# Second MLP of an attention, mixture-of-experts and MLP kernel: two tiles' activations turned on TensorE, the token rows of tiles 3 on turned through DRAM and 32x32 VectorE transposes

## The chip, the cores and the metric

One core of a Trainium2 chip runs the whole program. The time is the device time of one execution in microseconds (us), and the figure for a kernel is the median of its runs. The engines are TensorE (PE, with its weight loads shown apart as PEld), VectorE (DVE), ScalarE (ACT), GpSimd (POOL) and SyncE (SP, which only issues DMAs here). Each engine takes its instructions in the order in which the kernel writes them.

## The reference, cut to what matters

Attention comes first, then a layer of 8 experts with two of them for each token, then a second MLP over all 2304 tokens. The change touches the expert layer's last sum and the MLP:

```python
out[mask] += top2_w[mask, k, None] * (h @ w2[e])      # two expert rows for each token

h = x @ w_in                                          # 2304x512 @ 512x1024
e = np.exp(h - h_max)
sm = e / (np.sum(e, axis=-1, keepdims=True) + 1e-09)
solu = h * sm
mu, var = mean(solu), mean((solu - mu) ** 2)          # over the 1024 features
ln = (solu - mu) / np.sqrt(var + 1e-06) * g_ln
return ln @ w_out                                     # 2304x1024 @ 1024x512
```

All matrices are float32. The kernel splits each operand into a high and a low part (fp32r) and forms three products.

## The kernel before, in words

The 2304 tokens are 18 tiles of 128 tokens. In the MLP stage, a tile has its tokens on the 128 partitions and its features along the free dimension. A matrix product contracts over partitions, so both the tile's 512 input features and its 1024 activations have to be turned (features to partitions) before `h_in` and before `o_out`.

The stage is one loop over `i` (L1172). Each line of its body serves another tile, and nothing but the order written here sets the order on the engines (the schedule is manual):

- `h_in(i)` is 48 matmuls of 256 columns on PE (L840), into one of two PSUM buffers.
- `d_read(i-1)` reads the activations of tile i-1 back from DRAM with four DMAs on SP, so that each 32x32 block lies where a block transpose needs it. It waits until the write `d_write(i-1)` has landed.
- `d_back(i-2)` turns them: a DVE 32x32 block transpose of 128x1024 (L896), an ACT cast to the high part (L899), a DVE subtraction for the low part (L900).
- `x2_trans(i+1)` turns the input row of tile i+1: four PE transposes (L732), an ACT cast from PSUM (L734), a DVE subtraction (L735).
- `solu(i)` is a DVE maximum (L849), an ACT exponential (L852), a DVE product (L855), a DVE subtraction of the mean (L858), with small column operations (L853, L854, L856) between them.
- `d_write(i)` sends the result to DRAM.
- `combine(i+3)` adds the two expert rows of tile i+3: an ACT scaling (L822) and a DVE multiply-add (L823).
- `rstd(i-1)` is an ACT square with a sum (L868) and a chain of small DVE and ACT operations (L870 to L878).
- `o_out(i-3)` is 24 matmuls of 512 columns on PE (L923), an ACT copy out of PSUM (L928) and the store.
- `gather_y(i+5)` gathers expert rows with two indirect DMAs from POOL.

Tiles 16 and 17 do not go through DRAM: `d_trans` turns them with eight PE transposes each, two ACT casts (L913) and two DVE subtractions (L914), from activations that L860 has put in the column order of the DRAM path (partition 32g+c of chunk k holds feature 256g+32k+c). `w_out` is loaded in that order with four DMAs for each piece (L156); `w_in` is loaded in the plain order with one (L146). `combine(0)` to `combine(2)` and `x2_trans(0)`, `x2_trans(1)` stand ahead of the loop, between the last expert's products; `x2_trans(2)` stands in iteration 0.

Of the kernel before, what the change touches and what calls it, by code (L numbers as in the profile page):

```python
# [8 lines left out]
F32 = mybir.dt.float32  # L9
F32R = mybir.dt.float32r  # L10
# [10 lines left out]
NT, DM, FF, E = 2304, 512, 1024, 8  # L21
R = 4
NC = NT // 128
NL = S - 128 * R
KD, KF = DM // 128, FF // 128
# [22 lines left out]
def col_rows(t):  # L48

    j, c = divmod(t, 9)  # L50
    if c == 8:
        return [(64 * u, 64, (2 * j + u) * S + 128 * R, 1) for u in range(2)]
    return [(0, 128, (2 * j + c // R) * S + c % R, R)]

ORDER = """
F:100011101100000000100000000000101111 lk:0 lq:0 lkl:0 lk:1 kr:0 kmt:0 qm:0 lvl:0 km:0:0 klt:0 kl:0 km:0:1 kb:0
# [26 lines left out]
def attn_moe_kernel(ctx: ExitStack, tc: tile.TileContext, q, k, v, w_gate, w_noise, noise,  # L83
                    w1, w2, w_in, w_out, g_ln, out, order=None, stop=False):
    nc = tc.nc
    V, A, P, T, SP = nc.vector, nc.scalar, nc.gpsimd, nc.tensor, nc.sync
# [5 lines left out]
    dram = ctx.enter_context(tc.tile_pool(name="dram", bufs=1, space=DRAM))  # L92
    sb = ctx.enter_context(tc.tile_pool(name="sb", bufs=1))

    def slot(tag, shape, dt, name):
        return sb.tile(shape, dt, tag=tag, name=name)

    def ring(*tags):
        state = [-1]

        def take(shape, dt, name):
            state[0] = (state[0] + 1) % len(tags)
            return slot(tags[state[0]], shape, dt, name)
        return take

    new_raw = ring("R2", "R3", "R0", "R1")
    new_row = ring("S0", "S2", "S4", "S1", "S3")
    new_out = ring("S9", "S8", "S10")
    new_s2 = ring("S5", "S6", "S7", "S11")
# [6 lines left out]
    tab = dram.tile([OVT * 128, 2], I32, name="tab")  # L116
    win32 = dram.tile([DM, FF], F32, name="win32")
    wout32 = dram.tile([FF, DM], F32, name="wout32")
    dd = [dram.tile([128, FF], F32, name=f"dd{t}") for t in range(NC - 2)]

    def bank_t():
        return psT.tile([128, 512], F32, tag="t", name="t")
# [4 lines left out]
    def bank_b():  # L127
        return psB.tile([128, 512], F32, tag="b", name="b")
# [13 lines left out]

    def load_w1(e, j):
        t = new_raw([128, KD, 256], F32, "raw")
        src = win32 if e == E else w1[e]
        SP.dma_start(out=t, in_=src[:, 256 * j:256 * j + 256].rearrange("(k p) f -> p k f", p=128))  # L146
        raw[1, e, j] = t

    def load_w2(e, j):
# [116 lines left out]
    RH = {}  # L266
# [462 lines left out]
    def transpose_split(t, hi, lo):  # L729
        ps = bank_t()  # L730
        for kk in range(KD):
            T.transpose(ps[:, 128 * kk:128 * kk + 128], t[:, 128 * kk:128 * kk + 128], ident)  # L732
        pv = ps.rearrange("p (k t) -> p k t", k=KD)
        A.copy(hi, pv)  # L734
        V.tensor_sub(lo, pv, hi)  # L735
# [62 lines left out]
    yg, x2r, x2T, hb, dT, rsd = {}, {}, {}, {}, {}, {}  # L798
# [4 lines left out]
    def col_of(t):  # L803

        return t if t < NC - 2 else 2 * NC - 3 - t
# [13 lines left out]
    def combine(t):  # L819
        a, b = yg.pop((t, 0)), yg.pop((t, 1))  # L820
        c = col_of(t)
        A.activation(out=a, in_=a, func=AF.Copy, scale=gw[:, c, 0:1])  # L822
        V.scalar_tensor_tensor(a, b, gw[:, c, 1:2], a, op0=OP.mult, op1=OP.add)  # L823
        x2r[t] = a

    def x2_trans(t):
        a = x2r.pop(t)
        hi = new_s2([128, KD, 128], F32R, "x2h")
        lo = new_s2([128, KD, 128], F32R, "x2l")
        transpose_split(a, hi, lo)  # L830
        x2T[t] = (hi, lo)

    def h_in(t):
        hi, lo = x2T.pop(t)
        pa = bank_a()
        for n in range(2):
            for kk in range(KD):
                for s, (x, w) in enumerate(((hi, W1h), (hi, W1l), (lo, W1h))):
                    for c in range(2):
                        T.matmul(pa[:, n, 256 * c:256 * c + 256], lhsT=x[:, kk, :],  # L840
                                 rhs=w[2 * n + c][:, kk, :], start=(kk == 0 and s == 0 and c == 0),
                                 stop=(kk == KD - 1 and s == 2), skip_group_check=True)
        hb[t] = pa

    def solu(t):
        pa = hb.pop(t)
        c = col[:, t]
        pf = pa.rearrange("p n f -> p (n f)")
        V.reduce_max(c[:, 0:1], pf, axis=AX, negate=True)  # L849
        ed = new_ed([128, 2, FF], F32, "ed")  # L850
        e, d = ed[:, 0], ed[:, 1]
        A.activation(out=e, in_=pf, func=AF.Exp, bias=c[:, 0:1], accum_out=c[:, 1:2])  # L852
        V.tensor_scalar(c[:, 2:3], c[:, 1:2], 1e-9, None, op0=OP.add)  # L853
        V.reciprocal(c[:, 2:3], c[:, 2:3])  # L854
        V.scalar_tensor_tensor(d, pf, c[:, 2:3], e, op0=OP.mult, op1=OP.mult, accum_out=c[:, 3:4])  # L855
        V.tensor_scalar(c[:, 4:5], c[:, 3:4], -1.0 / FF, None, op0=OP.mult)  # L856
        if t < NC - 2:
            V.tensor_scalar(d, d, c[:, 4:5], None, op0=OP.add)  # L858
        else:
            V.tensor_scalar(e.rearrange("p (k g c) -> p g k c", g=4, k=KF), d.rearrange(  # L860
                "p (g k c) -> p g k c", g=4, k=KF), c[:, 4:5], None, op0=OP.add)
            e, d = d, e
        rsd[t] = e, d, c[:, 7:8]
# [20 lines left out]
    def d_write(t):  # L884
        SP.dma_start(out=dd[t], in_=rsd[t][1])

    def d_read(t):
        x = dq[t] = new_dq([128, 2, FF], F32, "dq")
        for g in range(4):
            SP.dma_start(out=x[32 * g:32 * g + 32, 0].rearrange("i (b f) -> i b f", b=4),  # L890
                         in_=dd[t].rearrange("(b i) f -> i b f", i=32)[:, :, 256 * g:256 * g + 256])

    def d_back(t):
        x = dq.pop(t)
        xt = x[:, 1].rearrange("p (k b i) -> p k b i", k=KF, b=4)
        V.transpose(xt.rearrange("p k b i -> p b k i"), x[:, 0].rearrange("p (b k c) -> p b k c", b=4, k=KF))  # L896
        xt = xt.rearrange("p k b i -> p k (b i)")
        dt = new_dT([128, 2, KF, 128], F32R, "dT")
        A.copy(dt[:, 0], xt)  # L899
        V.tensor_sub(dt[:, 1], xt, dt[:, 0])  # L900
        dT[t] = (dt[:, 0], dt[:, 1])

    def d_trans(t):
        d = rsd[t][1]
        dt = new_dT([128, 2, KF, 128], F32R, "dT")
        for i in range(2):
            ps = bank_t()
            for k in range(4):
                c = 512 * i + 128 * k
                T.transpose(ps[:, 128 * k:128 * k + 128], d[:, c:c + 128], ident)  # L910
            pv = ps.rearrange("p (k t) -> p k t", k=4)
            hi, lo = (dt[:, j, 4 * i:4 * i + 4, :] for j in range(2))
            A.copy(hi, pv)  # L913
            V.tensor_sub(lo, pv, hi)  # L914
        dT[t] = (dt[:, 0], dt[:, 1])

    def o_out(t):
        hi, lo = dT.pop(t)
        pb = bank_b()
        for kk in range(KF):  # L920
            wh, wl = (w[:, kk % 2, :] for w in WO[kk // 2])
            for s, (x, w) in enumerate(((hi, wh), (hi, wl), (lo, wh))):
                T.matmul(pb, lhsT=x[:, kk, :], rhs=w, start=(kk == 0 and s == 0),  # L923
                         stop=(kk == KF - 1 and s == 2))
        y = rsd.pop(t)[2]
        o = new_out([128, DM], F32, "o")
        if t < NC - 1:
            A.activation(out=o, in_=pb, func=AF.Copy, scale=y)  # L928
        else:
            A.activation(out=o[:, 0:256], in_=pb[:, 0:256], func=AF.Copy, scale=y)  # L930
            V.tensor_scalar(o[:, 256:512], pb[:, 256:512], y, None, op0=OP.mult)  # L931
        for p0, n, row, st in col_rows(col_of(t)):
            dst = out[row:row + n, :] if st == 1 else out[row - row % S:row - row % S + st * n, :].rearrange(
                "(p r) d -> p r d", r=st)[:, row % S, :]
            SP.dma_start(out=dst, in_=o[p0:p0 + n, :])
# [232 lines left out]
    x2_trans(1)  # L1168
    A.preload_act_table_set(ACT_SET)
    combine(2)  # L1170
    split_w2(E, 2)
    for i in range(NC + 3):  # L1172
        if i < NC:
            h_in(i)
        if 0 <= i - 1 < NC - 2:
            d_read(i - 1)
        if 0 <= i - 2 < NC - 2:
            d_back(i - 2)
        if 2 <= i < NC - 1:
            x2_trans(i + 1)  # L1180
        if i < NC:
            solu(i)
        if i < NC - 2:
            d_write(i)
        if i == 0:
            x2_trans(2)
        if i < NC - 3:
            combine(i + 3)
        if i == 1:
            split_w2(E, 3)  # L1190
        if 1 <= i <= NC:
            rstd(i - 1)
        if i >= 3:
            o_out(i - 3)
        if i in (NC - 1, NC):
            d_trans(i - 1)
        if i + 5 < NC:
            gather_y(i + 5)
# [31 lines left out]
```

## Time and profile before

| | |
|---|---|
| median of 3 runs | 815.04 us (814.2 to 815.2) |
| the profiled execution | 813.08 us, span 811.3 us |
| PE busy | 756.5 us, 93% of the span |
| PEld busy | 682.5 us, 84% |
| DVE busy | 504.0 us, 62% |
| ACT busy | 293.9 us, 36% |
| POOL busy | 147.1 us, 18% |
| granted TensorE clock, mean | 0.981 of 2.4 GHz |

The span runs from the first to the last instruction; the execution's time includes 1.8 us around it. A busy share is an average over stages. The MLP loop takes the last 220 us of the span.

### The profile page before, as it was taken

The page shows a single profiled execution, that of the slowest core. Times are in us where ns is not written, and L with a number is a line of the kernel's source. Part 1 is how long each engine was busy: PE and PEld are TensorE (multiplying, and loading weights), DVE is VectorE, ACT ScalarE, POOL GpSimd, SP SyncE. Part 2 cuts the span into 40 slices and gives each one's busy share as a digit, 9 for nine tenths or more (in the row PEclk, how much of TensorE's full clock was granted, in tenths as well). Part 3 has the DMA queues.
Part 4 walks back from the last instruction along what each step waited for, and adds up shares of the span by engine and source line. Part 5 has one row for each costly group of instructions (what it writes and reads, how often), then busy time and mean ns, then how long its engine had stood idle before and what let it go on. Part 6 is the DMA issues. An engine that isn't in the chain of part 4 may idle for free. (4 is left out here: it accounts for less than half of the span.)

```text
span 811.3 us, 12471 instructions
## 1 busy us (share of the span) xinstructions
PE 756.5 (93%) x4918; PEld 682.5 (84%) x4918; DVE 504.0 (62%) x884; ACT 293.9 (36%) x484; POOL 147.1 (18%) x130
## 2 busy tenths in 40 slices
PE   2877859999999999999999999999988999999997
PEld 1776858989889889899899899898777999899986
DVE  5899783335656656657646656555466777767661
ACT  1566531333223223223232332231444444444441
POOL 3584563020110110200100200000341211200000
PEclk9998899999999999999999999999997999999999
DMA  9973444264454443554544452532754645543311
GB/s 266 269 249 118 143 158 143 79 195 156 134 178 130 144 157 129 170 168 128 177 137 141 170 168 79 162 119 90 219 167 156 179 151 164 156 144 130 107 50 39
DMA packets 82974, 122.07 MB, mean 150 GB/s; under 512 B 15072, under 2 KB 53984, under 8 KB 82912
## 3 DMA queue, kind: packets, MB, share of 16 engines
q1 hardware_dynamic: 76832, 101.32, 39.3%
q0 software_dynamic: 6080, 19.93, 8.7%
q8 instruction: 39, 0.64, 0.3%
q14 instruction: 23, 0.19, 0.1%
HBM read 88.72 MB, written 32.51 MB: 149 GB/s over the span
## 5 line engine op out<-in xcount | busy, mean ns | idle before, releaser
L756 PE MATMUL a<-xh,w1h 128*128 128x320 f32 x448 | 138.6, 309 | 1.2 <-DVE hl L761 1.2
L756 PE MATMUL a<-xl,w1h 128*128 128x320 f32 x448 | 138.4, 309 | 0.0
L756 PE MATMUL a<-xh,w1l 128*128 128x320 f32 x448 | 138.4, 309 | 0.0
L792 PE MATMUL b<-w2h,hh 128*128 128x512 f32 x320 | 128.8, 402 | 0.0
L792 PE MATMUL b<-w2h,hl 128*128 128x512 f32 x320 | 126.7, 396 | 0.0
L792 PE MATMUL b<-w2l,hh 128*128 128x512 f32 x320 | 126.3, 395 | 0.0
L760 ACT ACTIVATE hh<-a 128x640 fp32r<-128x640 f32 x56 | 39.5, 706 | 159.9 <-PE a L756 159.9
L725 POOL DMA_INDIRECT xg<-xd,idx x38 | 40.7, 1070 | 304.1 <-PE t L732 294.7
L761 DVE SCALAR_TENSOR_TENSOR hl<-a,hh 128x640 fp32r<-128x640 f32 x56 | 46.1, 823 | 64.8 <-ACT hh L760 64.8
L756 PEld LDWEIGHTS a<-xh,w1h 128*128 128x128 f32 x448 | 84.1, 188 | 1.8 <-DVE hl L761 1.4
L756 PEld LDWEIGHTS a<-xl,w1h 128*128 128x128 f32 x448 | 84.1, 188 | 0.4
L756 PEld LDWEIGHTS a<-xh,w1l 128*128 128x128 f32 x448 | 84.2, 188 | 0.0
L815 POOL DMA_INDIRECT yg<-yd,posi x36 | 37.7, 1048 | 212.4 <-DVE w1l L162 100.1
L792 PEld LDWEIGHTS b<-w2h,hl 128*128 128x128 f32 x320 | 60.0, 187 | 13.9
L792 PEld LDWEIGHTS b<-w2l,hh 128*128 128x128 f32 x320 | 60.2, 188 | 13.0
L792 PEld LDWEIGHTS b<-w2h,hh 128*128 128x128 f32 x320 | 60.2, 188 | 12.6
L840 PE MATMUL a<-w1h,x2h 128*128 128x256 f32 x288 | 58.3, 284 | 7.8 <-ACT x2h L734 7.3
L162 DVE TENSOR_TENSOR w1l<-raw,w1h 128x1024 fp32r<-128x1024 f32 x32 | 38.9, 1222 | 33.5 <-ACT w1h L161 33.5
L840 PE MATMUL a<-w1h,x2l 128*128 128x256 f32 x288 | 57.8, 282 | 0.2 <-DVE x2l L735 0.2
L840 PE MATMUL a<-w1l,x2h 128*128 128x256 f32 x288 | 57.7, 282 | 0.0
L794 DVE COPY yo<-b 128x512 f32<-128x512 f32 x24 | 16.6, 691 | 64.2 <-PE b L792 64.2
L923 PE MATMUL b<-w2x,dT 128*128 128x512 f32 x216 | 54.4, 400 | 0.0
(209 smaller groups left out, 1395.1 us busy)
## 6 DMA issues: line engine op xcount, KB each, us to landing
raw<-in_moe_w_dram SPq DMA_DIRECT2D x64, 512.0 KB
yd<-yo SPq DMA_DIRECT2D x40, 256.0 KB
dd<-ed SPq DMA_DIRECT2D x16, 512.0 KB
dq<-dd SPq DMA_DIRECT2D x64, 128.0 KB
k<-in_k_dram SPq DMA_DIRECT2D x4, 1024.0 KB
q<-in_q_dram SPq DMA_DIRECT2D x4, 1024.0 KB
v<-in_v_dram SPq DMA_DIRECT2D x4, 1024.0 KB
xd<-xr SPq DMA_DIRECT2D x8, 512.0 KB
```

The source lines that it names most:

```text
L162: (pick_engine(20 + j, P, V) if e == 0 else V).tensor_sub(W1l[j], t, W1h[j])
L725: P.indirect_dma_start(out=t, out_offset=None, in_=xd[0:NRA, :] if first else xd, in_offset=bass.IndirectOffsetOnAxis(ap=idxA[:, a:a + 1] ...
L756: T.matmul(pa[:, n, 0:HC], lhsT=a, rhs=b, start=(kk == 0 and s == 0), stop=(kk == KD - 1 and s == 2))
L760: A.activation(out=h2, in_=pa[:, :, 0:HC], func=AF.Relu)
L761: V.scalar_tensor_tensor(l2, pa[:, :, 0:HC], 0.0, h2, op0=OP.max, op1=OP.subtract)
L792: T.matmul(pb, lhsT=x, rhs=y, start=(kk == 0 and s == 0), stop=(kk == KF - 1 and s == 2))
L794: (A.copy if a % 2 else V.tensor_copy)(t, pb)
L815: P.indirect_dma_start(out=r, out_offset=None, in_=yd[0:n, :], in_offset=bass.IndirectOffsetOnAxis(ap=posi[:, c, j:j + 1], axis=0))
L840: T.matmul(pa[:, n, 256 * c:256 * c + 256], lhsT=x[:, kk, :], rhs=w[2 * n + c][:, kk, :], start=(kk == 0 and s == 0 and c == 0), stop=(kk ...
L923: T.matmul(pb, lhsT=x[:, kk, :], rhs=w, start=(kk == 0 and s == 0), stop=(kk == KF - 1 and s == 2))
```

## The change

The constant `NP = 2` names the first tiles that skip DRAM on the activations' side. Four things change:

1. Activations of tiles 0 and 1 are turned by `d_trans` on PE (in iterations 1 and 2), as those of tiles 16 and 17 are. Their `d_write`, `d_read` and `d_back` go. `o_out(0)` and `o_out(1)` move one iteration earlier, to `i` = 2 and 3; iteration 4 has no `o_out`; from `i` = 5 on it is `o_out(i-3)` as before.
2. The combined rows of tiles 3 to 17 are written to DRAM (`xx`) after `combine`, read back in iteration i by `x2_read(i+2)` with four DMAs on SP, and turned in `x2_back(i+1)` by a DVE block transpose of 128x512, an ACT cast and a DVE subtraction. The four PE transposes of each of these tiles go.
3. The block order puts feature 128g+32k+c on partition 32g+c of chunk k, so `w_in` is loaded in that order, with four DMAs for each piece in place of one.
4. Tiles 0, 1 and 2 are still turned on PE; an ACT copy puts their columns in the same order first.

```diff
+NP = 2
-    dd = [dram.tile([128, FF], F32, name=f"dd{t}") for t in range(NC - 2)]
+    xx = {t: dram.tile([128, DM], F32, name=f"xx{t}") for t in range(3, NC)}
+    dd = {t: dram.tile([128, FF], F32, name=f"dd{t}") for t in range(NP, NC - 2)}
...
     def load_w1(e, j):
-        src = win32 if e == E else w1[e]
-        SP.dma_start(out=t, in_=src[:, 256 * j:256 * j + 256].rearrange("(k p) f -> p k f", p=128))
+        if e < E:
+            SP.dma_start(out=t, in_=w1[e][:, 256 * j:256 * j + 256].rearrange("(k p) f -> p k f", p=128))
+        else:
+            for g in range(4):
+                SP.dma_start(out=t[32 * g:32 * g + 32], in_=win32[128 * g:128 * g + 128, 256 * j:256 * j + 256].rearrange(
+                    "(k c) f -> c k f", c=32))
...
     def combine(t):
...
-        x2r[t] = a
+        if t in xx:
+            SP.dma_start(out=xx[t], in_=a)
+            return
+        p = x2r[t] = slot(f"RH{t}", [128, DM], F32, "x2p")
+        A.copy(p.rearrange("p (k g c) -> p g k c", g=4, k=KD), a.rearrange("p (g k c) -> p g k c", g=4, k=KD))
+
+    def x2_read(t):
+        x = x2r[t] = new_raw([128, 2, DM], F32, "xq")
+        for g in range(4):
+            SP.dma_start(out=x[32 * g:32 * g + 32, 0].rearrange("i (b f) -> i b f", b=4),
+                         in_=xx[t].rearrange("(b i) f -> i b f", i=32)[:, :, 128 * g:128 * g + 128])
+
+    def x2_back(t):
+        x = x2r.pop(t)
+        hi = new_s2([128, KD, 128], F32R, "x2h")
+        lo = new_s2([128, KD, 128], F32R, "x2l")
+        xt = x[:, 1].rearrange("p (k b i) -> p k b i", k=KD, b=4)
+        V.transpose(xt.rearrange("p k b i -> p b k i"), x[:, 0].rearrange("p (b k c) -> p b k c", b=4, k=KD))
+        xt = xt.rearrange("p k b i -> p k (b i)")
+        A.copy(hi, xt)
+        V.tensor_sub(lo, xt, hi)
+        x2T[t] = (hi, lo)
...
-        if t < NC - 2:
+        if NP <= t < NC - 2:
...
-        if 0 <= i - 1 < NC - 2:
+        if i == 1:
+            d_trans(0)
+        if NP <= i - 1 < NC - 2:
             d_read(i - 1)
-        if 0 <= i - 2 < NC - 2:
+        if 1 <= i < NC - 2:
+            x2_read(i + 2)
+        if NP <= i - 2 < NC - 2:
             d_back(i - 2)
         if 2 <= i < NC - 1:
-            x2_trans(i + 1)
+            x2_back(i + 1)
         if i < NC:
             solu(i)
-        if i < NC - 2:
+        if NP <= i < NC - 2:
             d_write(i)
...
-        if i >= 3:
+        if 2 <= i < 2 + NP:
+            o_out(i - 2)
+        if i >= 3 + NP:
             o_out(i - 3)
-        if i in (NC - 1, NC):
+        if i in (NP, NC - 1, NC):
             d_trans(i - 1)
```

## Rows read from the trace of the kernel before

**Rows 1.** Windows: length, busy us of each engine (count), PEclk, DMA share, GB/s.

```profile
631.45:767.80 136.35, 136.35 (x890) 123.67 (x889) 96.83 (x192) 64.67 (x119) 18.74 (x16) 1.00 0.46 145
...
612.00:617.30 5.30, 5.15 (x23) 4.85 (x24) 3.93 (x7) 2.85 (x5) 0.00 (x0) 0.50 0.31 99
```

**Rows 2.** Chain that ended last: start us, us, what.

```profile
...
626.49 5.55 PE a L840 x48
...
765.65 5.55 PE a L840 x48
...
777.19 5.63 PE a L840 x48
```

**Rows 3.** DVE groups, 631.45 to 767.80: count | busy us, mean ns | idle before <-releaser.

```profile
L900 DVE TENSOR_TENSOR dT<-dq,dT 128x1024 fp32r<-128x1024 f32 x12 | 14.7, 1225 | 13.4 <-ACT dT L899 13.4
...
L853 DVE TENSOR_SCALAR col<-col 128x1 f32<-128x1 f32 x12 | 1.9, 154 | 15.3 <-ACT ed L852 15.3
...
L875 DVE TENSOR_TENSOR col<-col 128x1 f32<-128x1 f32 x12 | 1.9, 159 | 6.0 <-ACT col L872 6.0
```

**Rows 4.** DVE timeline, one iteration: start us, us, instruction [idle before <-releaser].

```profile
665.15 1.25 DVE L896 STREAM_TRANSPOSE dq<-dq 128x1024 f32<-128x1024 f32 x1
667.51 1.23 DVE L900 TENSOR_TENSOR dT<-dq,dT 128x1024 fp32r<-128x1024 f32 x1 [1.11 <-ACT dT L899]
668.65 0.68 DVE L735 TENSOR_TENSOR x2l<-t,x2h 128x512 fp32r<-128x512 f32 x1
...
674.31 0.75 DVE L823 SCALAR_TENSOR_TENSOR yg<-yg,gw 128x512 f32<-128x512 f32 x1
674.97 0.15 DVE L870 TENSOR_SCALAR col<-col 128x1 f32<-128x1 f32 x1
...
676.38 1.25 DVE L896 STREAM_TRANSPOSE dq<-dq 128x1024 f32<-128x1024 f32 x1
```

**Rows 5.** ACT timeline, the same iteration.

```profile
666.43 1.05 ACT L899 CAST dT<-dq 128x1024 fp32r<-128x1024 f32 x1 [1.49 <-DVE dq L896]
```

**Rows 6.** PE timeline, one tile's row transposes and the matmul after them.

```profile
631.88 0.60 PE L732 MATMUL t<-ident,yg 128*128 128x128 f32 x4
632.24 2.09 PE L923 MATMUL b<-w2x,dT 128*128 128x512 f32 x8
```

**Rows 7.** Groups of 128x512 instructions, L211 of the whole kernel, others from 590 us.

```profile
L211 DVE TENSOR_TENSOR dec<-dec,dec 128x512 f32<-128x512 f32 x16 | 10.9, 681 | 0.0
...
L822 ACT ACTIVATE yg<-yg,gw 128x512 f32<-128x512 f32 x15 | 10.7, 713 | 0.0
...
L913 ACT CAST dT<-t 128x512 fp32r<-128x512 f32 x4 | 2.1, 588 | 0.0
```

**Rows 8.** PE timeline, the loop's iterations 2 and 3.

```profile
603.96 0.60 PE L732 MATMUL t<-ident,yg 128*128 128x128 f32 x4
611.87 0.79 PE L840 MATMUL a<-w1h,x2h 128*128 128x256 f32 x2 [7.31 <-ACT x2h L734]
```

**Rows 9.** DVE timeline, iterations 1, 2, 4 and 17.

```profile
598.83 1.22 DVE L849 TENSOR_REDUCE col<-a 128x1 f32<-128x1024 f32 x1
...
606.12 0.14 DVE L870 TENSOR_SCALAR col<-col 128x1 f32<-128x1 f32 x1
...
608.96 1.25 DVE L896 STREAM_TRANSPOSE dq<-dq 128x1024 f32<-128x1024 f32 x1 [1.46 <-DMA dq<-dd]
...
631.45 1.25 DVE L896 STREAM_TRANSPOSE dq<-dq 128x1024 f32<-128x1024 f32 x1
...
779.37 1.25 DVE L896 STREAM_TRANSPOSE dq<-dq 128x1024 f32<-128x1024 f32 x1
```

**Rows 10.** SP timeline: issue of tile 0's activation write and read-back.

```profile
597.68 0.34 SPq L885 DMA_DIRECT2D dd<-ed  x1
600.74 2.21 SPq L890 DMA_DIRECT2D dq<-dd  x4
```

**Rows 11.** Window in which PE sat idle 1.16 us.

```profile
200.00:205.00 5.00, 3.84 (x26) 3.58 (x25) 4.72 (x9) 0.70 (x1) 0.00 (x0) 1.00 0.02 7
```

## The prediction

> **What bounds the kernel now.** I read the page's busy shares first. They show a kernel bound by TensorE, with VectorE at 62%. Shares mix stages, so next come the windows of the loop. In iterations 4 to 15, 631.45 to 767.80, PE is busy in all 136.35 us at full clock, and DVE in 96.83 us, 71% [rows 1]. The chain that ended last says the same: it goes from PE to PE, 626.49 to 765.65 for 12 iterations, 11.60 us each, and from 777.19 (`h_in(17)`) to the end of the span it takes 34.1 us [rows 2].
>
> The reader should not stop there. DVE is idle 29% of that window, and the grouped rows say for whom: 13.4 us for the ACT cast in `d_back`, 15.3 us for the exponential in `solu`, 6.0 us for the small ACT steps in `rstd` [rows 3]. Busy 96.8 and these 34.7 make 131.5 of 136.35 us; most of the rest is a gap of some hundredths at each instruction. None of the three waits is a wait for PE or a DMA. DVE goes through its instructions in the order written, and ACT can only start each of these operations when DVE has given it its input. The two engines therefore form one chain that is nearly full. Its length in one iteration can be read off the timeline: from one 128x1024 transpose (L896) to the next it is 676.38 − 665.15 = 11.23 us [rows 4]. PE needs 11.60. **So the DVE–ACT chain has 0.37 us of slack in an iteration, not 29%.**
>
> The pieces of the 11.23 us, start to start [rows 4]: `d_back` 3.50 (665.15 to 668.65), the row's subtraction L735 and `solu` 5.66 (to 674.31), `combine` 0.66 (to 674.97), `rstd` 1.41 (to 676.38).
>
> **The change part by part.**
>
> *Transposes that leave PE.* Four take from 631.88 to 632.24, where the next matmul starts: 0.36 us a tile, 0.09 each [rows 6]. 15 tiles lose them: −5.4 us of PE work. Tiles 0 and 1 add 16 for their activations: +1.44. An iteration of PE falls to 11.60 − 0.36 = 11.24 us.
>
> *The same turn on DVE.* `x2_back` is a block transpose of 128x512, an ACT cast that needs its result, and a subtraction that needs the cast. Before, the cast followed `d_back`'s on ACT while DVE was at L900, so that the subtraction started as soon as L900 was through [rows 4]. Now all three come after L900 in DVE's order, and DVE has nothing to do while ACT casts. No row shows the transpose at 512. At 1024 it takes 1.245 us [rows 4]; the half is 0.62, and the longest nearby 512-wide operation is 0.75 (L823) [rows 4]. Two-input subtractions take 1.225 at 1024 [rows 3] and 0.681 at 512 [rows 7]; the same ratio gives 0.69, which I take. The cast takes 1.05 at 1024 [rows 5], so at least 0.52 at 512; the ACT scaling of an SBUF row of this size takes 0.71 [rows 7] and the cast from PSUM 0.588 [rows 7]; I take 0.59. The handovers are 0.035 us from DVE to ACT (L896 ends at 666.40, L899 starts at 666.43) and 0.03 back [rows 4, 5]. Together the addition is 0.69 + 0.035 + 0.59 + 0.03 = **1.35 us a tile**, between 1.21 and 1.53. The subtraction itself now reads SBUF, 0.681 [rows 7], and not PSUM, 0.68 [rows 4]: no difference.
>
> The chain's iteration is then 11.23 + 1.35 = **12.58 us**, against 11.24 on PE. DVE and ACT become the bound, and PE waits some 1.3 us in each iteration, for the cast and the subtraction of the next tile's row.
>
> *Head.* Up to the end of `h_in(1)`, at 603.96 − 5.55 = 598.41 [rows 2, 8], nothing on the path moves. The ACT copies for tiles 0 to 2 (at most 0.71 each [rows 7]) fall into ACT's idle time ahead of `h_in(0)` and during it; uncovered, the third would cost 0.7. The twelve more SP issues for `w_in` are about 0.55 us each (2.21 for four [rows 10]), 6.6 us of a queue that has the whole of the last expert's products; I take nothing.
>
> - Iteration 1: `d_trans(0)` runs on PE from 598.41; its first four transposes are through at 599.0 (0.60 [rows 8]), a cast takes 0.59 [rows 7], two subtractions 0.60 start to start. The maximum that stood at 598.83 comes at 600.8, +2.0. `rstd(0)` is through at 606.12 + 1.41 + 2.0 = 609.5 [rows 4, 9].
> - Iteration 2: `d_back(0)` is gone, and with it PE's wait of 7.31 us [rows 8]. `x2_back(3)` needs its row read back. Its write goes out at 598.9, lands after 3.06 (597.68 to 600.74 [rows 10]), and a read-back took at most 8.2 us (600.74 to 608.96 [rows 9, 10]) with twice the bytes: 610.2 at the latest, against 609.5 when DVE is free. I take 609.5; the bound is +0.7. Then 1.35 + 5.66 + 0.66 + 1.41 = 9.08: 618.6. `d_trans(1)`'s casts stand behind the copy of `o_out(0)` on ACT; they and the two subtractions add 1.6: 620.2.
> - Iteration 3 has no `d_back`: 629.3.
>
> Before, iteration 4 began on DVE at 631.45 [rows 9]. It begins 2.2 us earlier. PE is some 10 us ahead by then (7.31 us of wait, and 5.3 us at clock 0.50 [rows 1], worth 2.65), but it can't use that: `h_in(5)` needs `x2_back(5)`.
>
> *The loop.* Iterations 4 to 14 are 11 × 12.58 = 138.4; 15 and 16 have no `combine`, 11.92 each. Iteration 17 begins at 629.3 + 138.4 + 23.8 = 791.5 on DVE, before at 779.37 [rows 9]: +12.1.
>
> *Tail.* `h_in(17)` follows `x2_back(17)`, which is in iteration 16 (from 779.6): 779.6 + 3.50 + 0.725 + 0.59 = 784.4 for the high part. After four matmuls it waits about 0.6 for the low part. From there to the end PE's work is unchanged, 34.1 [rows 2]: 819.1. `d_trans(16)` and `d_trans(17)` now meet an ACT that is later than before (the copy of `o_out(14)` only after `rstd(16)`); by the same pieces this just fits, and I keep 1 us for it in the range.
>
> Span 819.1 and 1.8 around it is 820.9 for the profiled execution, 7.8 above its 813.1. The median of the runs lies 2.0 above that execution: **823 us**. The bounds of the cast and transpose over 14 iterations are −2.0 and +2.5, those of head and tail −1.5 and +2: the likeliest case's own range is 819 to 828.
>
> **Rivals.**
>
> *A. VectorE has the room, and TensorE stays the bound.* For it: DVE is busy 71% of the window [rows 1]. The time would fall by the wait of 7.31, the 2.65 at half clock and 5.4 of transposes, less 1.44 for those added: 13.9 us, so 801. For this the chain would have to fit into 11.24 us, while it takes 11.23 without the addition. The tie with the kernel before comes at an addition of 1.35 − 8/15 = 0.82 us for each of the 15 tiles: the kernel is not slower if ACT's cast costs DVE nothing and the transpose under 0.8. The rows speak against it: the same pattern in `d_back` makes DVE wait 13.4 us in 12 iterations [rows 3].
>
> The Trainium skill (Perfetto Trace Analysis, Identifying the Most-Contended Engine) tells the reader to find the bottleneck by occupancy, and calls occupancy a fair measure of VectorE and ScalarE. By that rule an engine at 71% takes another 0.69 us in an iteration easily, and the time is that of A, 801. The waits of [rows 3] disagree with it here.
>
> *B. Tie.* The addition comes out near 0.82, or the head gives 8 us more than I counted: 813.4 to 816.7.
>
> *C. PE's clock falls in the new gaps.* After the wait of 7.31 us the clock was 0.50 for 5.3 us [rows 1, 8]. If a gap of 1.3 us did the same, an iteration of PE would be 11.24 + 2.65 = 13.9, longer than the chain's 12.58; 13 iterations are up to 17 us more. When PE is the bound the gaps close and the clock returns, so a part of this: 828 to 838. Against it: an idle 1.16 us left the clock at 1.00 [rows 11].
>
> That the turn does not leave PE can't be: those instructions are no longer written.
>
> **How the numbers follow.** Forecast 0.77, A 0.08, B 0.06, C 0.09. Predicted 823. The range 816.5 to 829 holds nearly all of the forecast, the upper edge of B and the lower edge of C, about 8 in 10. Slower by over 0.2% (what a measurement of this kernel can tell from no change, 1.6 us) is the forecast and C, 0.86; within 0.2% is B, 0.06; faster is A, 0.08.
>
> **What would show it.** In the profile after: 15 DVE transposes of 128x512 at 0.62 to 0.75 us, each followed by a DVE wait of about 0.65 for ACT; 12.4 to 12.8 us from one 128x1024 transpose to the next; PE waiting in nearly every iteration for `x2_back`'s cast and subtraction, at a clock of 1.00; the 7.31 us wait gone; iteration 4 beginning on DVE near 629 and iteration 17 near 791. I am wrong if the 1024-wide transposes stand closer than 11.9 us apart, if PE shows no waits between 640 and 780, or if PE's waits there name a DMA or a PSUM buffer and not `x2_back`.

## The result, and the profile after

The changed kernel takes 823.58 us (median; 823.19 to 824.04), the kernel before 814.62: a ratio of 1.012, with a 95% interval of 1.0101 to 1.014 (the two medians alone give 1.011). It is slower by 9 us; 823 was forecast.

The page of the changed kernel shows little of it (busy us, share of the span, instructions):

```profile
PE 762.1 (93%) x4874; PEld 681.1 (83%) x4874; DVE 511.5 (62%) x899; ACT 297.1 (36%) x489; POOL 145.6 (18%) x130
```

VectorE's share is 62% as before. The window of iterations 4 to 15, from the start of one 128x1024 transpose to that of the twelfth after it (columns as in [rows 1]), says more:

```profile
631.35:782.65 151.30, 138.61 (x859) 120.85 (x858) 104.89 (x204) 64.88 (x118) 13.98 (x14) 0.99 0.54 168
```

Twelve iterations took 136.35 us [rows 1] and now take 151.30, and PE, which was busy throughout, is now idle for 12.7 us of them. DVE's busy share has *fallen*, from 71% to 69%, while DVE, with its waits for ACT, became the bound. The groups of DVE instructions in that window (columns as in [rows 3]) show where its time goes:

```profile
L928 DVE TENSOR_TENSOR dT<-dq,dT 128x1024 fp32r<-128x1024 f32 x12 | 14.7, 1225 | 13.4 <-ACT dT L927 13.4
...
L848 DVE STREAM_TRANSPOSE xq<-xq 128x512 f32<-128x512 f32 x12 | 8.5, 704 | 0.0
L851 DVE TENSOR_TENSOR x2l<-xq,x2h 128x512 fp32r<-128x512 f32 x12 | 8.3, 692 | 8.2 <-ACT x2h L850 8.2
...
L881 DVE TENSOR_SCALAR col<-col 128x1 f32<-128x1 f32 x12 | 1.9, 154 | 15.3 <-ACT ed L880 15.3
...
L903 DVE TENSOR_TENSOR col<-col 128x1 f32<-128x1 f32 x12 | 1.9, 160 | 6.0 <-ACT col L900 6.0
```

The three waits for ACT of [rows 3] stand there unchanged: 13.4, 15.3 and 6.0 us. New are the transpose (L848, 8.5 us) and a fourth wait for ACT of 8.2 us. Busy 104.9 and waits 42.9 are 147.8 of 151.3 us. One iteration on DVE, which answers to [rows 4]:

```profile
669.26 1.25 DVE L924 STREAM_TRANSPOSE dq<-dq 128x1024 f32<-128x1024 f32 x1
671.62 1.23 DVE L928 TENSOR_TENSOR dT<-dq,dT 128x1024 fp32r<-128x1024 f32 x1 [1.12 <-ACT dT L927]
672.77 0.70 DVE L848 STREAM_TRANSPOSE xq<-xq 128x512 f32<-128x512 f32 x1
674.15 0.69 DVE L851 TENSOR_TENSOR x2l<-xq,x2h 128x512 fp32r<-128x512 f32 x1 [0.68 <-ACT x2h L850]
...
681.89 1.25 DVE L924 STREAM_TRANSPOSE dq<-dq 128x1024 f32<-128x1024 f32 x1
```

and ACT's two casts in it, which answer to [rows 5]:

```profile
670.54 1.05 ACT L927 CAST dT<-dq 128x1024 fp32r<-128x1024 f32 x1 [1.49 <-DVE dq L924]
673.50 0.62 ACT L850 CAST x2h<-xq 128x512 fp32r<-128x512 f32 x1 [1.91 <-DVE xq L848]
```

The reader is to follow the handovers. The activations' cast (L927) runs while DVE waits, the activations' subtraction (L928) while ACT waits. Then DVE transposes the row, from 672.77, while ACT still has nothing to do, and ACT casts it, from 673.50, while DVE has nothing to do until 674.15. From one 128x1024 transpose to the next it is 681.89 − 669.26 = 12.63 us, against 11.23 before.

PE's waits in the same twelve iterations (what waited, for what, us in total, times, longest):

```profile
PE a L868 <- ACT x2h L850: 12.7, 11, 3.6
```

All are for `x2_back`'s cast, none for a DMA or a PSUM buffer.

### The profile page after: what moved, and what is told of

Its sections match the earlier page's. It is cut to its first block, busy times and chain, and to the rows that moved or that the text cites. A ratio compares the mean times of both kernels' runs of the same rounds, so it can differ in the third digit from the quotient of the medians.

```text
span 822.2 us, 12535 instructions
## 1 busy us (share of the span) xinstructions
PE 762.1 (93%) x4874; PEld 681.1 (83%) x4874; DVE 511.5 (62%) x899; ACT 297.1 (36%) x489; POOL 145.6 (18%) x130
## 5 line engine op out<-in xcount | busy, mean ns | idle before, releaser
L822 POOL DMA_INDIRECT yg<-yd,posi x36 | 36.0, 1001 | 207.7 <-DVE w1l L169 100.3
L799 PEld LDWEIGHTS b<-w2h,hl 128*128 128x128 f32 x320 | 59.9, 187 | 13.9
L868 PEld LDWEIGHTS a<-w1h,x2h 128*128 128x128 f32 x288 | 44.6, 191 | 19.3 <-ACT x2h L850 18.4
```

Of the source, the lines that this page charges most:

```text
L799: T.matmul(pb, lhsT=x, rhs=y, start=(kk == 0 and s == 0), stop=(kk == KF - 1 and s == 2))
L822: P.indirect_dma_start(out=r, out_offset=None, in_=yd[0:n, :], in_offset=bass.IndirectOffsetOnAxis(ap=posi[:, c, j:j + 1], axis=0))
```

## The experiments

The theory: DVE and ACT form one in-order chain, in which each waits while the other works, and the change lengthened it past TensorE's 11.24 us an iteration. Its rivals: the trip through DRAM or SP's queue sets the pace; only the busy time of the new DVE instruction counts; TensorE's clock suffers from the gaps. Experiments 1 to 4 and 5 to 7 were measured in two later sets, in which the kernel before took 813.67 and 813.75 us. Each ratio is to the kernel before in the same set, and a difference of two times from different sets is uncertain by about 1 us.

**1. The same work, interleaved.** `d_back` and `x2_back` are split, so that both transposes come before both subtractions:

```diff
     def x2_back(t):
...
-        V.tensor_sub(lo, xt, hi)
         x2T[t] = (hi, lo)
+        return lambda: V.tensor_sub(lo, xt, hi)
...
+        late = []
         if NP <= i - 2 < NC - 2:
-            d_back(i - 2)
+            late.append(d_back(i - 2))
         if 2 <= i < NC - 1:
-            x2_back(i + 1)
+            late.append(x2_back(i + 1))
+        for f in late:
+            f()
```

Each helper now does its transpose and its cast and returns its subtraction, which runs later (`d_back` is changed in the same way, not shown).

> The changed kernel with one order altered: in an iteration DVE does the 128x1024 transpose, then the 128x512 transpose, then the two subtractions; ACT does the two casts in the same order. Work, DMAs and sizes are the same. Theory (DVE and ACT are one in-order chain, and the change lengthened it by 1.36 us for each tile, 0.60 for the transpose and 0.75 for a wait for ACT's cast): the 128x512 transpose fits into the wait of 1.11 us for the other cast, the row's cast runs during the other subtraction, so the iteration falls from 12.63 back to about 11.25 us, as long as TensorE's 11.24; 13 iterations are 17 us: about 806 us. Rival 1 (the round trip through DRAM, or the SP queue, sets the pace): nothing changes, 823. Rival 2 (it is only the added busy time of 0.70 us on DVE that costs): 11.9 us an iteration, 814.

Measured: 804.53 us (ratio to before 0.9902, 0.9877 to 0.9926), 18 to 19 us less than the changed kernel, with the same instructions and the same DMAs. One iteration on DVE:

```profile
674.86 1.25 DVE L924 STREAM_TRANSPOSE dq<-dq 128x1024 f32<-128x1024 f32 x1
676.03 0.67 DVE L848 STREAM_TRANSPOSE xq<-xq 128x512 f32<-128x512 f32 x1
677.22 1.23 DVE L929 TENSOR_TENSOR dT<-dq,dT 128x1024 fp32r<-128x1024 f32 x1 [0.52 <-ACT dT L927]
678.37 0.69 DVE L852 TENSOR_TENSOR x2l<-xq,x2h 128x512 fp32r<-128x512 f32 x1
...
686.10 1.25 DVE L924 STREAM_TRANSPOSE dq<-dq 128x1024 f32<-128x1024 f32 x1
```

The row's transpose (L848) now starts while ACT does the activations' cast, and the wait before L929 shrinks from 1.12 to 0.52 us; the row's subtraction (L852) waits for nothing. The iteration is 11.24 us. The addition of 1.4 us has gone without any work having gone. The window of the same twelve iterations:

```profile
629.91:764.46 134.55, 132.40 (x859) 119.94 (x858) 103.47 (x203) 63.72 (x118) 14.18 (x14) 1.00 0.59 189
```

DVE is now busy 77% of it, more than in either kernel, and the program is faster than both. What is left of PE's waits in the loop stands at its beginning:

```profile
PE a L868 <- ACT x2h L850: 1.6, 1, 1.6
PE b L951 <- issue: 0.9, 1, 0.9
PE b L951 <- ACT dT L941: 0.7, 1, 0.7
PE a L868 <- DVE x2l L852: 0.6, 1, 0.6
```

**2. The row's transpose first.** Transpose of the row, transpose of the activations, then the two subtractions. This hides the cast, and leaves the transpose in the chain.

```diff
+        late = []
+        if 2 <= i < NC - 1:
+            late.append(x2_back(i + 1))
         if NP <= i - 2 < NC - 2:
-            d_back(i - 2)
...
+            late.insert(0, d_back(i - 2))
+        for f in late:
+            f()
```

> The changed kernel with another order: 128x512 transpose first, then the 128x1024 transpose, then the subtraction for the activations, then that for the row. ACT's cast of the row runs during the longer transpose, so its wait is gone, but the DVE transpose itself stays in the chain. Theory: the addition falls from 1.36 to 0.60 us a tile, an iteration takes 11.85 us, 13 of them 10 us less than 12.63: about 813.5 us, near the tie with the kernel before that the prediction put at an addition of 0.82. Rival 1 (DRAM trip or SP queue): 823. Rival 2 (only DVE's busy time costs): no change either, 823.

Measured: 812.02 us (0.9983, 0.9971 to 0.9995). One iteration on DVE:

```profile
678.26 0.71 DVE L848 STREAM_TRANSPOSE xq<-xq 128x512 f32<-128x512 f32 x1
678.90 1.20 DVE L924 STREAM_TRANSPOSE dq<-dq 128x1024 f32<-128x1024 f32 x1
681.22 1.23 DVE L929 TENSOR_TENSOR dT<-dq,dT 128x1024 fp32r<-128x1024 f32 x1 [1.11 <-issue]
682.36 0.69 DVE L852 TENSOR_TENSOR x2l<-xq,x2h 128x512 fp32r<-128x512 f32 x1
...
690.09 0.71 DVE L848 STREAM_TRANSPOSE xq<-xq 128x512 f32<-128x512 f32 x1
```

690.09 − 678.26 = 11.83 us: the new wait is gone, and 0.60 us over the 11.23 of before is left, the row's transpose (0.64 start to start). The wait of 1.11 us is that for the activations' cast, as in the kernel before: ACT does it from 680.14 to 681.19. So of the addition of 1.4 us some 0.6 was the transpose and 0.8 the wait for the cast. The prediction's tie with the kernel before, at an addition of 0.82 us a tile, lies on the right side of this run: at 0.60 the kernel is just faster than before, by 1.65 us (the prediction's own sum, 15 tiles at 0.82 − 0.60, would have it faster by 3.3).

**3. The first part alone,** on the kernel before:

```diff
+NP = 2
...
+        if i == 1:
+            d_trans(0)
-        if 0 <= i - 1 < NC - 2:
+        if NP <= i - 1 < NC - 2:
...
+        if 2 <= i < 2 + NP:
+            o_out(i - 2)
...
-        if i in (NC - 1, NC):
+        if i in (NP, NC - 1, NC):
```

> The kernel before with the first part of the change alone: activations of tiles 0 and 1 turned on TensorE, their products one iteration earlier; token rows turned on TensorE as before. Theory: the wait of 7.31 us and the half clock after it (2.65 us) go, 1.44 us of transposes come, and the DVE-ACT chain at 11.23 us stays below TensorE's 11.60: 8.5 us less than before, about 806. Rival (this part is worth only the 2.2 us by which it brings DVE forward): 812.

Measured: 807.28 us (0.9927, 0.9905 to 0.9949), 6.4 less than before in the same set, against 8.5 expected. Its window of iterations 4 to 15:

```profile
627.91:762.77 134.86, 134.19 (x891) 122.09 (x890) 96.41 (x192) 63.42 (x118) 15.18 (x16) 1.00 0.49 145
```

PE is busy in all but 0.7 us of 134.86: TensorE is the bound again, and 6.4 of the 8.5 us that the head was to save arrive at the end. PE still waits 1.3 us around tiles 4 and 5, which the estimate left out; the other 0.8 us of the 2.1 missing stay unexplained.

**4. The second part alone:** the changed kernel with

```diff
-NP = 2
+NP = 0
...
-        if i == 1:
-            d_trans(0)
...
-        if i in (NP, NC - 1, NC):
+        if i in (NC - 1, NC):
```

> The changed kernel with the constant for the first tiles at 0: token rows of tiles 3 on through DRAM and DVE transposes, but the activations of tiles 0 and 1 through DRAM as before. Theory: the chain grows by 1.36 us in each of 15 iterations, and 0.37 us of slack in each is all that absorbs it; iteration 4 begins on DVE near 634 us and iteration 17 near 797: 826 to 828, so that the first part is worth only 2 to 4 us beside the second. Rival (both parts add up: the first gives 8.5 us whatever the second does): 832.

Measured: 829.42 us (1.0196, 1.0172 to 1.022), between the two expectations. The miss is at the head. The first and the third 128x1024 transpose of this kernel (iterations 2 and 4):

```profile
612.49 1.25 DVE L924 STREAM_TRANSPOSE dq<-dq 128x1024 f32<-128x1024 f32 x1 [4.63 <-DMA dq<-dd]
...
637.80 1.25 DVE L924 STREAM_TRANSPOSE dq<-dq 128x1024 f32<-128x1024 f32 x1
```

DVE waits 4.63 us for the read-back of tile 0's activations, where the kernel before waited 1.46 [rows 9], and iteration 4 begins at 637.8, not near 634. The DMA engines are at their fullest there. The window of 604.00 to 612.50 us, in this kernel and then in the kernel before (columns as in [rows 1]; the DMA share is the number before the last):

```profile
604.00:612.50 8.50, 0.67 (x6) 0.47 (x5) 3.26 (x10) 1.14 (x4) 3.05 (x4) 0.78 1.05 242
```

```profile
604.00:612.50 8.50, 1.19 (x9) 0.95 (x8) 5.28 (x11) 2.10 (x6) 2.92 (x3) 0.68 0.89 265
```

A share of 1.05, against 0.89. The gathers, the activations' trip and the rows' trip meet there. SP's queue is not what delays the read-back: SP begins to issue it at 601.44, before at 600.74, and ahead of the row's; but from there to DVE's transpose it takes 11.0 us, before 8.2. That the load on the DMA engines is what does it is likely, and not tried by itself.

So beside the second part the first is worth 829.4 − 823.6 = 5.8 us (6.8 when each is taken against the kernel before in its own set), and not 2 to 4. Alone it was worth 6.4 (experiment 3). The two parts add up after all, as the rival had it, but from 6.4 us and not from 8.5: the first part also takes two tiles' activations out of the DMA queues when these are fullest, which the expectation left out.

**5. The traffic without its use.** The first part alone, and the rows written and read back as in the change, with nobody using them.

```diff
...
+        if t in xx:
+            SP.dma_start(out=xx[t], in_=a)
+
+    def x2_read(t):
+        x = new_raw([128, 2, DM], F32, "xq")
...
+        if 1 <= i < NC - 2:
+            x2_read(i + 2)
```

> The first part alone (token rows turned on TensorE), and beside it the second part's traffic: rows of tiles 3 on are written to DRAM and read back with the same DMAs on SP, but nothing uses what is read back. Theory (the DVE-ACT chain is the cost): as the first part alone, 806 to 809. Rival (the added DMAs cost time by load or in SP's queue): more than 809, up to 823.

Measured: 807.35 us (0.9921, 0.9905 to 0.9938), as the first part alone (807.28; both 6.4 us below the kernel before of their own set). On DVE the 128x1024 transposes stand as without the traffic:

```profile
651.92 1.25 DVE L906 STREAM_TRANSPOSE dq<-dq 128x1024 f32<-128x1024 f32 x1 [0.41 <-issue]
...
663.16 1.25 DVE L906 STREAM_TRANSPOSE dq<-dq 128x1024 f32<-128x1024 f32 x1
...
674.40 1.25 DVE L906 STREAM_TRANSPOSE dq<-dq 128x1024 f32<-128x1024 f32 x1
```

11.24 us each. With the first part in place, the traffic costs nothing that these runs can tell.

**6. The transpose twice.** The DVE transpose of each row stands there a second time.

```diff
         V.transpose(xt.rearrange("p k b i -> p b k i"), x[:, 0].rearrange("p (b k c) -> p b k c", b=4, k=KD))
+        V.transpose(xt.rearrange("p k b i -> p b k i"), x[:, 0].rearrange("p (b k c) -> p b k c", b=4, k=KD))
```

> The changed kernel with the 128x512 DVE transpose of each row done twice, the second time over the first. Theory: DVE is the bound, so each of the 15 tiles takes 0.60 us more, start to start: about 9 us, 832. Rival (TensorE's clock or the DMAs set the pace and DVE has room): 823 to 825.

Measured: 833.33 us (1.0249, 1.023 to 1.0269), 9.75 more than the changed kernel (10.6 when each is taken against the kernel before in its own set).

```profile
670.43 1.25 DVE L925 STREAM_TRANSPOSE dq<-dq 128x1024 f32<-128x1024 f32 x1
...
673.93 0.70 DVE L848 STREAM_TRANSPOSE xq<-xq 128x512 f32<-128x512 f32 x1
674.67 0.71 DVE L849 STREAM_TRANSPOSE xq<-xq 128x512 f32<-128x512 f32 x1
676.07 0.69 DVE L852 TENSOR_TENSOR x2l<-xq,x2h 128x512 fp32r<-128x512 f32 x1 [0.69 <-ACT x2h L851]
...
683.81 1.25 DVE L925 STREAM_TRANSPOSE dq<-dq 128x1024 f32<-128x1024 f32 x1
```

The second transpose starts 0.74 us after the first, not 0.60 (it reads and writes the same tile; whether that is the reason was not tried), and the iteration takes 683.81 − 670.43 = 13.38 us, 0.75 more than the changed kernel's. Over 13 or 14 iterations that is 9.8 to 10.5 us: the time follows DVE's chain.

**7. Another wait filled.** The interleaved kernel, with `combine` between `solu`'s maximum and its exponential:

```diff
         V.reduce_max(c[:, 0:1], pf, axis=AX, negate=True)
+        if t < NC - 3:
+            combine(t + 3)
...
-        if i < NC - 3:
-            combine(i + 3)
```

> The interleaved kernel (804.5 us) with the sum of the two expert rows moved ahead: ACT scales before the exponential, and DVE adds while ACT computes it. Theory: this 0.66 us goes into DVE's wait of 1.27 us, the chain falls from 11.24 to 10.6 us, below TensorE's 11.24; TensorE's waits for tile 5's row (1.55 and 0.60 us) go or shrink: 801.5 to 804. Rival (ACT's scaling delays the exponential by its 0.71 us): 804.5 or more.

Measured: 802.14 us (0.9865, 0.9839 to 0.9892).

```profile
670.18 1.25 DVE L926 STREAM_TRANSPOSE dq<-dq 128x1024 f32<-128x1024 f32 x1
...
675.42 0.74 DVE L830 SCALAR_TENSOR_TENSOR yg<-yg,gw 128x512 f32<-128x512 f32 x1
676.78 0.15 DVE L883 TENSOR_SCALAR col<-col 128x1 f32<-128x1 f32 x1 [0.61 <-ACT ed L882]
...
680.76 1.25 DVE L926 STREAM_TRANSPOSE dq<-dq 128x1024 f32<-128x1024 f32 x1
```

The sum (L830) runs while ACT computes the exponential, the wait after it is 0.61 us and no longer 1.27, and the iteration takes 680.76 − 670.18 = 10.58 us on DVE, below TensorE's 11.24. This is the fastest of the versions, 1.35% below the kernel before. Its interval and that of the interleaved kernel overlap (0.9839 to 0.9892 and 0.9877 to 0.9926), so that it beats that one is likely and not shown.

Put in order of what DVE's chain takes in an iteration (us from one iteration's first transpose to the next's):

```
kernel                         DVE chain   median us
interleaved, combine early       10.58       802.1
interleaved                      11.24       804.5
row's transpose first            11.83       812.0
the changed kernel               12.63       823.6
transpose twice                  13.38       833.3
```

From 11.24 us on, which is also TensorE's share of an iteration, each microsecond of the chain costs 12.7 to 14.5 us from row to row, for 13 or 14 iterations that go through it. Below it, little is left to gain.

## Why the prediction was right

*What bounds the kernel.* Right, and it decided the sign. Rival A, which took VectorE's idle share for room, put this kernel at 801 us. Experiments 1, 2 and 6 show that the chain's length sets the time. DVE's busy share doesn't tell: it is 69% in the changed kernel and 77% in the faster interleaved one. Rival A's sum for TensorE was not far off. With the chain shortened below TensorE's share, in experiment 7, the kernel takes 802.1, 11.6 us less than before where A had 13.9; what A lacked was that room on VectorE.

*The addition.* Taken as 1.35 us, measured 674.15 − 672.77 = 1.38 to the start of the subtraction. The transpose takes 0.704 us (0.69 taken), the cast 0.62 (0.59 taken, from a cast that reads PSUM; this one reads SBUF). The subtraction from SBUF takes 0.69, as from PSUM. The iteration is 12.63 us against 12.58 forecast.

*The head.* Iteration 1's maximum, the transposes of rows 3 and 4 and iteration 4 on DVE, which answer to [rows 9]:

```profile
603.12 1.22 DVE L877 TENSOR_REDUCE col<-a 128x1 f32<-128x1024 f32 x1
...
611.58 0.71 DVE L848 STREAM_TRANSPOSE xq<-xq 128x512 f32<-128x512 f32 x1
...
622.22 0.70 DVE L848 STREAM_TRANSPOSE xq<-xq 128x512 f32<-128x512 f32 x1
...
631.35 1.25 DVE L924 STREAM_TRANSPOSE dq<-dq 128x1024 f32<-128x1024 f32 x1
```

All four come 2.0 to 2.3 us after the times forecast (600.8, 609.5, 620.2, 629.3). The row of tile 3 is back in time: its transpose at 611.58 waits for nothing. The lateness is there from the start: `h_in(0)` starts at 588.76, before at 586.60. Counted from there, iteration 4 begins after 42.6 us against 42.7 forecast. The change doesn't show as its cause. Of the 2.2 us, 1.7 are there when the expert products of 320 columns begin (178.6 us, before 176.9), in code that the change leaves alone. And among the nine profiled executions the six with the ACT copies and the new `w_in` loads start `h_in(0)` between 586.22 (experiment 6) and 588.76, the three without them between 586.60 and 588.21 (experiment 5). What makes one execution late is not shown: between 100 and 150 us the granted clock was 0.86 in this execution and 0.93 in the one before, but 0.86 too in that of the interleaved kernel, which starts `h_in(0)` at 587.40.

*The loop.* Iteration 17 begins on DVE at 794.62, 163.3 us after iteration 4; 162.2 were forecast.

*The tail.* The chain that ended last is PE's from `h_in(17)` on:

```profile
787.56 6.18 PE a L868 x48
793.74 5.59 PE b L951 x24
799.33 0.87 PE t L938 x8
800.20 5.56 PE b L951 x24
805.76 1.13 PE t L938 x8
806.90 11.20 PE b L951 x48
```

`h_in(17)` takes 6.18 us, 0.55 more than before (5.63 [rows 2]): its weight load waits 0.2 us for the low part, and the rest shows as slower first matmuls. The forecast had 0.6 for the low part. `d_trans(17)` takes 1.13 and not 0.87, since it waits for DVE to read its PSUM buffers. From the start of `h_in(17)` to the end of the span it is 34.6 us, against 34.7 forecast.

*The sum.* The span is 822.2 us, 3.1 over the 819.1 forecast: 2.05 of them at the head, 1.1 in the loop, none in the tail. The median is only 0.6 over the forecast, and that is in part luck. The forecast added 2.0 us because the profiled execution of the kernel before lay that far under its median; the profiled execution of the changed kernel (823.92) started its loop late and lies 0.3 above its median. The two nearly cancel. Between the kernels 8.0 us were forecast (823 − 815.04) and 9.0 measured; the loop's 1.1 us is that difference.

*The gaps and the clock.* PE waits 0.85 to 0.97 us for each row's cast from `h_in(7)` to `h_in(16)`, and the rest of the 1.39 us (12.63 − 11.24) shows as a wait of 0.2 us for the low part, at the weight load, and slower first matmuls. Of the new gaps in the loop only the one of 3.58 us, ahead of `h_in(5)`, was followed by a lower clock:

```profile
636.20:641.00 4.80, 4.74 (x26) 4.54 (x27) 3.41 (x6) 2.86 (x6) 0.00 (x0) 0.67 0.51 150
```

0.67 is a mean over 4.8 us: 2.4 GHz at first, then 1.2 GHz from about 637.8 to 641.2. Nothing came of it, since PE was not the bound: DVE's next iterations take 12.64 and 12.63 us. The shorter gaps left the clock at 1.00, so rival C did not happen here. What it fears can happen, though. In experiment 6 PE is idle for 1.73 us ahead of 662.72, and soon after it the clock is at 1.2 GHz:

```profile
664.00:667.00 3.00, 3.00 (x17) 3.00 (x16) 1.66 (x4) 2.44 (x4) 0.00 (x0) 0.50 0.02 7
```

Later gaps there of up to 2.07 us left it at 1.00. DVE's iterations go on at 13.37 and 13.38 us through that stretch: the lower clock cost nothing while the chain was the bound.

*What was taken as nothing.* The ACT copies and the `w_in` loads show no cost in the start of `h_in(0)` beyond the spread of the executions (586.22 to 588.76 with them, 586.60 to 588.21 without). They were not tried by themselves. The rows' DMAs were taken at nothing in the loop, and experiment 5 bears this out; at the head experiment 4 shows that they have a price when the activations of tiles 0 and 1 go through DRAM too. The prediction had no term for that, and the change itself did not need one.

## What to carry to other kernels

Two engines that handed work to each other in program order acted here as one resource. Add up the busy time and the waits for each other from the start of an instruction to its next occurrence, and hold that, not the busy share, against the bound. When work is moved off the busiest engine, look at how its new instructions lie between those waits. Here the same instructions cost 9 us when written one helper after the other and gained 9 when the two helpers' transposes were put side by side.

## What the runs showed that was not expected

A DVE transpose right behind another one overlapped its end in experiment 2 (0.64 us start to start for a duration of 0.71), but not in experiment 6, where it reads and writes the same tile as that one (0.74 for 0.70). That this is the reason was not tried. And the rows' DMA trips, which cost nothing in the loop, made DVE wait 3.2 us longer at the head in experiment 4, where the gathers and the activations' trips stand in the queues too (a DMA share of 1.05, against 0.89 in the kernel before).
